# Eight starting places modulo 256 bytes for the streamed and weight tiles of an MLP

## The chip, the cores and the metric

The kernel runs on one core of a Trainium2 chip. The metric is device time in microseconds (us) for one execution. The time before is the median of three runs, 1006.82 us (1005.56 to 1008.35).

## What is computed

The reference is a linear attention with exponential features (8 batches, 8 heads, 576 tokens, head size 64, 128 features), followed by an MLP on 4608 tokens of width 512:

```python
proj = einsum('bhsd,md->bhsm', x * scale, omega)
phi  = exp(h - max(h)) / sqrt(m)         # h = proj - |x|^2 / 2, for q and for k
kv   = einsum('bhsm,bhsd->bhmd', phi(k), v)
attn = einsum('bhsm,bhmd->bhsd', phi(q), kv) / (phi(q) . sum(phi(k)) + 1e-06)
h    = x @ w_in                          # 4608 x 512 by 512 x 2048
g    = where(h > 0, h, exp(min(h, 0)) - 1)
out  = g @ w_out                         # 4608 x 2048 by 2048 x 512
```

The MLP is the larger part. To keep precision its operands are split into a high and a low part of type fp32r, and each product is computed as three: high by high, high by low, low by high.

## The kernel before, in words

Tokens are cut into 9 blocks of 512 (`TB`). The hidden width 2048 is cut into 16 slices of 128 (`NF`). A *step* is one block with one slice: `layer1` makes the slice of the hidden layer and `layer2` adds its product to the block's output. Both layers are written as products of three matmuls.

In `layer1` (from line 1000) the stationary operand, the weights that are loaded into the array, is a 128x128 piece of w1 in the buffer `w1c`; the operand that streams is 512 tokens of `xh` or `xl`, the attention's output, held in a ring of 1536 tokens. There are 4 products of three (lines 1012 to 1014), over the width 512, into one PSUM bank. ScalarE and VectorE then make `e` from it (lines 1021 to 1025), and the high and low parts of `g` are cut from `e` (helpers at lines 403 and 406). In `layer2` the stationary operand is a 128x128 piece of `g`, and what streams is a row of 512 of `w2l` or `w2h`; 4 products of three (lines 1050 to 1052) go to four banks. So each step is 24 matmuls of 512 columns, and there are 9 x 16 = 144 steps.

Where the tiles lie: `const` holds tiles of the whole run (identity, `ones`, `of`, `om`, `kvs`, then `w2h`, `w2l`, `xh`, `xl`), all of a size that is a multiple of 256 bytes in each partition. Then comes a pad of 48 floats (`GAP`), then the pool `mv` with two buffers of `w1c` and two of `g`, each 4096 bytes, then a pad of 16 floats, then the pool `sb` with all the rest, among it the tiles `tk` and `tq` (line 568 loads them as weights while `om` streams, 256 columns). A tile's start is rounded up to 32 bytes.

`weights` (line 976) fills `w1c`. In the first block's steps the weights come as 64-bit numbers and are converted by ScalarE and VectorE (`from_f64`), then stored to the scratch `w1s` in the chip's main memory (line 990); in all later blocks they are loaded from there by one DMA of 512 KB (line 993). SP's queue issues all DMAs.

The order of all the work on every engine is set ahead of time by a planner (`Plan.order`): each operation has an engine, an assumed duration and a due time, and the planner starts the one due first among those whose inputs and buffers are ready. It knows nothing of the addresses of tiles. Attention for later blocks is interleaved with the MLP of earlier ones until about 800 us; after that the MLP is alone.

Of the kernel before, what the change touches and what calls it, by code (L numbers as in the profile page):

```python
# [9 lines left out]
F32 = mybir.dt.float32  # L10
# [9 lines left out]
P = 128  # L20
# [9 lines left out]
NTT = TB // P  # L30
NBLK = NTOK // TB
RING = 3 * TB
GAP = 48
GR = 64
NJ = 9
NV = 10 * (D + 1)
# [305 lines left out]
def performer_elu_kernel(  # L342
# [39 lines left out]
    nc.vector.memset(kvs[0], 1.0)  # L382
    nc.vector.tensor_copy(ones, kvs[0])

    w2h = const.tile([P, NF, DM], F32R, name="w2h")
    w2l = const.tile([P, NF, DM], F32R, name="w2l")
    w1s = dram.tile([NF, P, 2 * NC * P], F32, name="w1s")
    part = dram.tile([NHALF * TB, DM], F32, name="part")
    turned = [dram.tile([P, NQB * NJ * QB], F32, name=f"turned{n}") for n in range(NTURN)]
    xh = const.tile([P, NC, RING], F32R, name="xh")  # L390
    xl = const.tile([P, NC, RING], F32R, name="xl")

    const.tile([P, GAP], F32, name="gap0")
    sb.tile([P, 64 - GAP], F32, name="gap1")

    pl = Plan()
    op = pl.op
# [515 lines left out]
    def from_f64(src, hi, lo, nm, due, key):  # L913

        raw = Buf(sb, [P, 2 * 512], I32, "raw", f"raw_{nm}", 3)
        u = Buf(sb, [P, 512], F32, "u", f"u_{nm}", 3)

        def words():
            return raw().rearrange("p (n w) -> p n w", w=2)

        def low():
            return words()[:, :, 0]

        def up():  # L930
            return words()[:, :, 1]

        def ui():
            return u().bitcast(I32)

        def tail():
            return u().bitcast(U16).rearrange("p (n w) -> p n w", w=2)[:, :, 0]


        op(  # L940
            "SP", 500, due - 10, lambda: nc.sync.dma_start(raw(), src), (), ((raw, 0), (raw, 1)), P * 4096,
            after=due - EARLY,
        )
        op(
            "ACT", 571, due - 7,
            lambda: nc.scalar.activation(u(), up().bitcast(F32), AF.Copy, scale=2.0 ** -112), ((raw, 1),), (u,),
        )
        op(
            "DVE", dve(512, True), due - 6,
            lambda: nc.vector.tensor_scalar(u(), u(), -F64_MAX, F64_MAX, ALU.max, ALU.min), (u,), (u,), port=True,  # L950
        )
        op(
            "DVE", dve(512, True), due - 6,
            lambda: nc.vector.tensor_scalar(ui(), ui(), 3, 0x7FFFFFFF, ALU.logical_shift_left, ALU.bitwise_and),
            (u,), (u,), port=True,
        )
        op(
            "DVE", dve(512), due - 6,
            lambda: nc.vector.scalar_tensor_tensor(ui(), up(), -(2 ** 31), ui(), ALU.bitwise_and, ALU.bitwise_or),
            (u, (raw, 1)), (u,), port=True,  # L960
        )
        op(
            "DVE", dve(512), due - 5,
            lambda: nc.vector.scalar_tensor_tensor(tail(), low().bitcast(U32), 2.0 ** -29, tail(), ALU.mult, ALU.add),  # L964
            (u, (raw, 0)), (u,),
        )
        op(
            "ACT", act(512), due - 4, lambda e: copy(e, hi(), u()), (u,), (key + ("h",),),
            alt=other("conv_hi", "DVE", dve(512, True)), port=True,
        )  # L970
        op(
            "DVE", dve(512), due - 3,
            lambda e: tt(e, lo(), u(), hi().bitcast(F32), ALU.subtract), (u, key + ("h",)), (key + ("l",),),
            alt=other("conv_sub", "POOL", pool(512)), port=True,
        )

    w1c, gt, acc = {}, {}, {}

    def weights(F, due):

        blk, f = STEPS[F][:2]
        t = w1c[F] = Buf(mv, [P, 2, NC * P], F32R, "w1c", f"w1c_{F}", 2)

        def flat():
            return t().rearrange("p a c -> p (a c)").bitcast(F32)

        both = ((t, "h"), (t, "l"))
        if blk == 0:
            from_f64(w1[f], lambda: t()[:, 0], lambda: t()[:, 1], f"w1_{f}", due, (t,))
            op("SP", 500, due, lambda: nc.sync.dma_start(w1s[f], flat()), both, (("w1s", f),), P * 4096)  # L990
            from_f64(w2[f], lambda: w2h[:, f], lambda: w2l[:, f], f"w2_{f}", due + CONV1 - (CONV2 if f < SPLIT[1] else CONV3), ("w2", f))
        else:
            op("SP", 500, due - 8, lambda: nc.sync.dma_start(flat(), w1s[f]), (("w1s", f),), both, P * 4096)

    def ring(blk):

# [2 lines left out]
    def layer1(F, due):  # L999
        blk, f = STEPS[F][:2]  # L1000
        o = (blk * TB) % RING
        w = w1c.pop(F)
        p = Buf(ps, [P, 512], F32, "pa", f"ph_{F}", 4)
        e = Buf(sb, [P, TB], F32, "e", f"e_{F}", 2)
        g = gt[F] = Buf(mv, [P, 2, TB], F32R, "g", f"g_{F}", 2)

        def ph():
            return p()[:, 0:TB]

        def mms(c):  # L1010
            wh, wl = w()[:, 0, c * P:(c + 1) * P], w()[:, 1, c * P:(c + 1) * P]
            nc.tensor.matmul(ph(), wh, xh[:, c, o:o + TB], start=(c == 0), stop=False)  # L1012
            nc.tensor.matmul(ph(), wh, xl[:, c, o:o + TB], start=False, stop=False)  # L1013
            nc.tensor.matmul(ph(), wl, xh[:, c, o:o + TB], start=False, stop=(c == NC - 1))  # L1014

        for c in range(NC):
            reads = [(z, k) for k in ring(blk) if k[1] == c for z in ("xh", "xl")]
            op("PE", mm(TB, 3), due + 0.5 * c, lambda c=c: mms(c), [*reads, (w, "h"), (w, "l")], (p,))
        due += 2

        op("ACT", act(TB, True), due, lambda: nc.scalar.activation(e(), ph(), AF.Relu, scale=-1.0), (p,), (e,))  # L1021
        op("ACT", act(TB), due + 0.2, lambda: nc.scalar.activation(e(), e(), AF.Exp, scale=-1.0), (e,), (e,))  # L1022
        op(
            "DVE", dve(TB), due + 0.8,
            lambda: nc.vector.scalar_tensor_tensor(e(), e(), -1.0, ph(), ALU.add, ALU.max), (p, e), (e,),  # L1025
        )
        first, second = ("ACT", act(TB)), ("DVE", dve(TB, True))
        if blk:
            first, second = second, first
        op(*first, due + 1.2, lambda x: copy(x, g()[:, 0], e()), (e,), ((g, 0),), alt=other("g_hi", *second), port=True)  # L1030

        first, second = ("POOL", pool(TB)), ("DVE", dve(TB))
        if not blk:
            first, second = second, first
        op(
            *first, due + 1.5,
            lambda x: tt(x, g()[:, 1], e(), g()[:, 0].bitcast(F32), ALU.subtract), (e, (g, 0)), ((g, 1),),
            alt=other("g_lo" if blk else "g_lo0", *second), port=True,
        )

    def layer2(F, due):
        blk, f, f0, f1 = STEPS[F]
        g = gt.pop(F)
        for tt in range(NTT):
            if f == f0:
                acc[tt] = Buf(ps, [P, DM], F32, f"acc{tt}", f"acc_{blk}_{f0}_{tt}", 1)

            def mms(tt=tt, a=acc[tt]):
                ts = slice(tt * P, (tt + 1) * P)
                nc.tensor.matmul(a(), g()[:, 0, ts], w2l[:, f], start=(f == f0), stop=False)  # L1050
                nc.tensor.matmul(a(), g()[:, 0, ts], w2h[:, f], start=False, stop=False)  # L1051
                nc.tensor.matmul(a(), g()[:, 1, ts], w2h[:, f], start=False, stop=(f == f1 - 1))  # L1052

            d = due + 0.65 * tt
            op("PE", 3 * 229, d, mms, ((g, 0), (g, 1), ("w2", f, "h"), ("w2", f, "l")), (acc[tt],))
            if f < f1 - 1:
                continue
            o = Buf(sb, [P, DM], F32, "u", f"o_{blk}_{f0}_{tt}", 3)
            r = blk * TB + tt * P
            if f0:  # L1060
                op("SP", 500, d - 10, lambda o=o, r=r: nc.sync.dma_start(o(), part[r:r + P]), (("part", r),), (o,), P * DM * 4)
                op(
                    "DVE", dve(DM), d,
                    lambda o=o, a=acc[tt]: nc.vector.tensor_tensor(o(), a(), o(), ALU.add), (acc[tt], o), (o,),
                )
            else:
                op(
                    "ACT", act(DM, True), d, lambda e, o=o, a=acc[tt]: copy(e, o(), a()), (acc[tt],), (o,),
                    alt=other("out", "DVE", dve(DM)),
                )  # L1070
            dst, keys = (out, ()) if f1 == NF else (part, (("part", r),))
            op("SP", 500, d + 1, lambda o=o, r=r, dst=dst: nc.sync.dma_start(dst[r:r + P], o()), (o,), keys, P * DM * 4)
# [129 lines left out]
```

## Time and profile before

| | |
|---|---|
| median of three runs | 1006.82 us (1005.56 to 1008.35) |
| the profiled execution | 1004.03 us, its span 1002.3 us |
| busy PE, VectorE (DVE), ScalarE (ACT), GpSimd (POOL) | 987.3, 708.5, 667.4, 189.6 us |
| chain that ended last | PE 86%, DVE 6%, DMA 4%, ACT 3% |
| bytes moved | 179.12 MB, 179 GB/s on the mean |

Busy time of an engine is the time with at least one of its instructions open. Matmuls overlap in the profile, since each is open from its start until its result is through, and the ends are modelled; so the sum of PE's durations is larger than its busy time, and the distance between starts says more than the duration. PEld is the loading of weights, which overlaps the matmuls. A line of a group gives the line of the code, the engine, the operation, out<-in, shapes, the count, then busy time in us and the mean duration of one in ns, then the idle time of the engine just before them and what ended it.

### The profile page before, as it was taken

The page shows a single profiled execution, that of the slowest core. Times are in us where ns is not written, and L with a number is a line of the kernel's source. Part 1 is how long each engine was busy: PE and PEld are TensorE (multiplying, and loading weights), DVE is VectorE, ACT ScalarE, POOL GpSimd, SP SyncE. Part 2 cuts the span into 40 slices and gives each one's busy share as a digit, 9 for nine tenths or more (in the row PEclk, how much of TensorE's full clock was granted, in tenths as well). Part 3 has the DMA queues.
Part 4 walks back from the last instruction along what each step waited for, and adds up shares of the span by engine and source line. Part 5 has one row for each costly group of instructions (what it writes and reads, how often), then busy time and mean ns, then how long its engine had stood idle before and what let it go on. Part 6 is the DMA issues. An engine that isn't in the chain of part 4 may idle for free.

```text
span 1002.3 us, 17185 instructions
## 1 busy us (share of the span) xinstructions
PE 987.3 (99%) x5230; PEld 805.7 (80%) x5230; DVE 708.5 (71%) x2511; ACT 667.4 (67%) x1716; POOL 189.6 (19%) x223
## 2 busy tenths in 40 slices
PE   9899999999999999999999999999999999999998
PEld 8688788787878887887788788888788778888886
DVE  6999999988887777786777776777776532333332
ACT  8988768997777777886787687777776422122222
POOL 3323201332222221222122122222122100000000
PEclk9999999999999999999999999999999999999999
DMA  8576775777666645754575556664574243324321
GB/s 202 162 228 209 240 261 195 249 249 246 221 204 197 206 146 160 250 180 144 180 242 187 175 179 208 197 206 148 165 224 153 94 125 131 100 98 134 105 85 63
DMA packets 66572, 179.12 MB, mean 179 GB/s; under 512 B 9456, under 2 KB 21936, under 8 KB 66480
## 3 DMA queue, kind: packets, MB, share of 16 engines
q1 hardware_dynamic: 66480, 178.03, 56.5%
q8 instruction: 42, 0.69, 0.3%
q14 instruction: 50, 0.41, 0.1%
HBM read 143.92 MB, written 34.08 MB: 178 GB/s over the span
## 4 chain that ended last, share of the span: by engine, by line
PE 86%; DVE 6%; DMA 4%; ACT 3%; issue 1%; POOL 0%; SPq 0%; DVEq 0%; ACTq 0%; POOLq 0%
PE ph L1012 12%; PE acc L1050 12%; PE acc L1051 12%; PE ph L1013 12%; PE acc L1052 12%; PE ph L1014 12%; PE ppq L568 2%; PE ppk L568 2%; PE pn L704 2%; PE ppq L518 1%; DMA part<-o 1%; PE ppk L518 1%; DVE u_w L964 1%; PE pkv L623 1%; ACT hk L490 1%
## 5 line engine op out<-in xcount | busy, mean ns | idle before, releaser
L1012 PE MATMUL ph<-xh,w1c 128*128 128x512 f32 x576 | 228.7, 397 | 1.2 <-DVE e L1025 1.1
L1050 PE MATMUL acc<-w2l,g 128*128 128x512 f32 x576 | 228.1, 396 | 0.0
L1013 PE MATMUL ph<-xl,w1c 128*128 128x512 f32 x576 | 226.2, 393 | 0.0
L1051 PE MATMUL acc<-w2h,g 128*128 128x512 f32 x576 | 226.0, 392 | 0.0
L1052 PE MATMUL acc<-w2h,g 128*128 128x512 f32 x576 | 225.4, 391 | 0.0
L1014 PE MATMUL ph<-xh,w1c 128*128 128x512 f32 x576 | 225.3, 391 | 0.0
L1021 ACT ACTIVATE e<-ph 128x512 f32<-128x512 f32 x144 | 85.9, 596 | 198.1 <-PE ph L1014 197.4
L1025 DVE SCALAR_TENSOR_TENSOR e<-e,ph 128x512 f32<-128x512 f32 x144 | 98.3, 683 | 110.6 <-ACT e L1022 109.6
L406 POOL TENSOR_TENSOR hq<-hq,den 128x512 f32<-128x512 f32 (+1 forms) x96 | 81.5, 860 | 288.0 <-DVE den L788 75.0
L1012 PEld LDWEIGHTS ph<-xh,w1c 128*128 128x128 f32 x576 | 108.3, 188 | 26.3 <-issue 2.7
L1014 PEld LDWEIGHTS ph<-xh,w1c 128*128 128x128 f32 x576 | 108.2, 188 | 24.5
L1052 PEld LDWEIGHTS acc<-w2h,g 128*128 128x128 f32 x576 | 108.2, 188 | 24.4
L1050 PEld LDWEIGHTS acc<-w2l,g 128*128 128x128 f32 x576 | 108.3, 188 | 21.2 <-issue 0.9
L1013 PEld LDWEIGHTS ph<-xl,w1c 128*128 128x128 f32 x576 | 108.3, 188 | 18.0
L1051 PEld LDWEIGHTS acc<-w2h,g 128*128 128x128 f32 x576 | 108.3, 188 | 18.0
L403 DVE CAST g<-e 128x512 fp32r<-128x512 f32 x128 | 55.4, 433 | 72.8 <-PE acc L1052 69.9
L406 DVE TENSOR_TENSOR g<-e,g 128x512 fp32r<-128x512 f32 x144 | 100.2, 696 | 2.0
L1022 ACT ACTIVATE e<-e 128x512 f32<-128x512 f32 x144 | 91.2, 633 | 2.8
L577 ACT ACTIVATE p2q<-ppq,sqq 128x128 f32<-128x128 f32 x216 | 66.5, 366 | 27.6 <-PE ppq L568 24.0
L788 DVE CUSTOM_DVE_ANT_0 junk<-hq,pz 128x128 f32<-128x128 f32 (+1 forms) x320 | 74.5, 280 | 6.0 <-PE pz L767 4.8
L586 DVE CUSTOM_DVE_ANT_0 hq<-ppq,p2q 128x128 f32<-128x128 f32 x216 | 54.4, 285 | 32.1 <-ACT p2q L577 31.5
L577 ACT ACTIVATE p2k<-ppk,sqk 128x128 f32<-128x128 f32 x216 | 66.6, 365 | 13.4 <-DVE mnk L586 7.6
(175 smaller groups left out, 1407.7 us busy)
## 6 DMA issues: line engine op xcount, KB each, us to landing
w1c<-w1s SPq DMA_DIRECT2D x128, 512.0 KB, 3.8
raw_w<-in_w_dram SPq DMA_DIRECT2D x32, 512.0 KB, 4.4
xk<-in_kx_dram SPq DMA_DIRECT2D x24, 576.0 KB, 5.0
xq<-in_qx_dram SPq DMA_DIRECT2D x24, 576.0 KB, 3.8
turned<-tb SPq DMA_DIRECT2D x24, 576.0 KB, 4.4
qh<-turned SPq DMA_DIRECT2D x96, 144.0 KB, 4.8
v<-in_v_dram SPq DMA_DIRECT2D x32, 325.0 KB, 5.2
out_dram<-o SPq DMA_DIRECT2D x36, 256.0 KB, 2.4
```

The costliest lines, as they stand in the source:

```text
L406: (nc.vector if e == "DVE" else nc.gpsimd).tensor_tensor(*args)
L577: nc.scalar.activation(p2()[:, a], view()[:, a, M:], AF.Identity, bias=sq()[:, j:j + 1], scale=1.0)
L788: nc.vector.tensor_tensor_reduce(out=junk()[r], in0=h()[r, j, :], in1=pz()[r, a * P:(a + 1) * P], scale=1.0, scalar=EPS, op0=ALU.mult, op1 ...
L1012: nc.tensor.matmul(ph(), wh, xh[:, c, o:o + TB], start=(c == 0), stop=False)
L1013: nc.tensor.matmul(ph(), wh, xl[:, c, o:o + TB], start=False, stop=False)
L1014: nc.tensor.matmul(ph(), wl, xh[:, c, o:o + TB], start=False, stop=(c == NC - 1))
L1021: op("ACT", act(TB, True), due, lambda: nc.scalar.activation(e(), ph(), AF.Relu, scale=-1.0), (p,), (e,))
L1022: op("ACT", act(TB), due + 0.2, lambda: nc.scalar.activation(e(), e(), AF.Exp, scale=-1.0), (e,), (e,))
L1025: lambda: nc.vector.scalar_tensor_tensor(e(), e(), -1.0, ph(), ALU.add, ALU.max), (p, e), (e,),
L1050: nc.tensor.matmul(a(), g()[:, 0, ts], w2l[:, f], start=(f == f0), stop=False)
L1051: nc.tensor.matmul(a(), g()[:, 0, ts], w2h[:, f], start=False, stop=False)
L1052: nc.tensor.matmul(a(), g()[:, 1, ts], w2h[:, f], start=False, stop=(f == f1 - 1))
```

## The change

Five pads in `const` take the place of the two pads. They stand ahead of `w2h`, between `w2h` and `w2l`, ahead of `xh`, between `xh` and `xl`, and behind `xl`. The buffers of `w1c` and `g` become flat tiles of 1048 floats (`SPAN`), 4192 bytes: the high half has the first 512, then 8 floats (`SHIFT`) are left free, then come the low half's 512, and 16 more are left free. So the low half begins 32 bytes further modulo 256 than the high one, and the second buffer 96 bytes further than the first. The DMAs of `w1c` have two pieces of 2048 bytes in each partition, where they had one of 4096. All else stays.

```diff
-GAP = 48
+SHIFT = 8
+SPAN = 2 * (512 + SHIFT) + SHIFT
...
+    def pad(n, name):
+        const.tile([P, n], F32, name=name)
+
+    pad(32, "gap0")
     w2h = const.tile([P, NF, DM], F32R, name="w2h")
+    pad(20, "gap1")
     w2l = const.tile([P, NF, DM], F32R, name="w2l")
...
+    pad(44, "gap2")
     xh = const.tile([P, NC, RING], F32R, name="xh")
+    pad(56, "gap3")
     xl = const.tile([P, NC, RING], F32R, name="xl")
-
-    const.tile([P, GAP], F32, name="gap0")
-    sb.tile([P, 64 - GAP], F32, name="gap1")
+    pad(24, "gap4")
...
+    def halves(t):
+        return t()[:, 0:2 * (512 + SHIFT)].rearrange("p (a c) -> p a c", a=2)[:, :, 0:512]
...
-        t = w1c[F] = Buf(mv, [P, 2, NC * P], F32R, "w1c", f"w1c_{F}", 2)
+        t = w1c[F] = Buf(mv, [P, SPAN], F32R, "w1c", f"w1c_{F}", 2)
...
-            op("SP", 500, due - 8, lambda: nc.sync.dma_start(flat(), w1s[f]), (("w1s", f),), both, P * 4096)
+            op("SP", 500, due - 8, lambda: nc.sync.dma_start(both_parts(), w1s[f].rearrange("p (a c) -> p a c", a=2)), (("w1s", f),), both, P * 4096)
...
-        g = gt[F] = Buf(mv, [P, 2, TB], F32R, "g", f"g_{F}", 2)
+        g = gt[F] = Buf(mv, [P, SPAN], F32R, "g", f"g_{F}", 2)
...
-            wh, wl = w()[:, 0, c * P:(c + 1) * P], w()[:, 1, c * P:(c + 1) * P]
+            wh, wl = halves(w)[:, 0, c * P:(c + 1) * P], halves(w)[:, 1, c * P:(c + 1) * P]
...
-                nc.tensor.matmul(a(), g()[:, 0, ts], w2l[:, f], start=(f == f0), stop=False)
-                nc.tensor.matmul(a(), g()[:, 0, ts], w2h[:, f], start=False, stop=False)
-                nc.tensor.matmul(a(), g()[:, 1, ts], w2h[:, f], start=False, stop=(f == f1 - 1))
+                nc.tensor.matmul(a(), halves(g)[:, 0, ts], w2l[:, f], start=(f == f0), stop=False)
+                nc.tensor.matmul(a(), halves(g)[:, 0, ts], w2h[:, f], start=False, stop=False)
+                nc.tensor.matmul(a(), halves(g)[:, 1, ts], w2h[:, f], start=False, stop=(f == f1 - 1))
```

## Rows read from the trace of the kernel before

**Rows 1.** The page: busy time of PE, and the granted clock in 40 slices.

```profile
PE 987.3 (99%) x5230; PEld 805.7 (80%) x5230; DVE 708.5 (71%) x2511; ACT 667.4 (67%) x1716; POOL 189.6 (19%) x223
...
PEclk9999999999999999999999999999999999999999
```

**Rows 2.** The page: the chain that ended last, by engine.

```profile
PE 86%; DVE 6%; DMA 4%; ACT 3%; issue 1%; POOL 0%; SPq 0%; DVEq 0%; ACTq 0%; POOLq 0%
```

**Rows 3.** Groups of PE over the whole span, by line.

```profile
L1012 PE MATMUL ph<-xh,w1c 128*128 128x512 f32 x576 | 228.7, 397 | 1.2 <-DVE e L1025 1.1
L1050 PE MATMUL acc<-w2l,g 128*128 128x512 f32 x576 | 228.1, 396 | 0.0
L1013 PE MATMUL ph<-xl,w1c 128*128 128x512 f32 x576 | 226.2, 393 | 0.0
L1051 PE MATMUL acc<-w2h,g 128*128 128x512 f32 x576 | 226.0, 392 | 0.0
L1052 PE MATMUL acc<-w2h,g 128*128 128x512 f32 x576 | 225.4, 391 | 0.0
L1014 PE MATMUL ph<-xh,w1c 128*128 128x512 f32 x576 | 225.3, 391 | 0.0
```

**Rows 4.** Timeline of PE in the tail (start, duration in us): first and last of 105.

```profile
899.62 0.39 PE L1050 MATMUL acc<-w2l,g 128*128 128x512 f32 x1
...
923.43 0.39 PE L1052 MATMUL acc<-w2h,g 128*128 128x512 f32 x1
```

**Rows 5.** Groups of PE from 820 to 980 us, the MLP alone.

```profile
L1012 PE MATMUL ph<-xh,w1c 128*128 128x512 f32 x119 | 46.6, 392 | 0.0
L1013 PE MATMUL ph<-xl,w1c 128*128 128x512 f32 x118 | 46.5, 394 | 0.0
L1014 PE MATMUL ph<-xh,w1c 128*128 128x512 f32 x119 | 46.2, 388 | 0.0
L1051 PE MATMUL acc<-w2h,g 128*128 128x512 f32 x115 | 45.3, 394 | 0.0
L1050 PE MATMUL acc<-w2l,g 128*128 128x512 f32 x115 | 45.1, 392 | 0.0
L1052 PE MATMUL acc<-w2h,g 128*128 128x512 f32 x115 | 44.6, 388 | 0.0
```

**Rows 6.** The tile w1c: durations min/median/max in ns, first and last start.

```profile
L1013 PE MATMUL ph<-xl,w1c x576: 387/394/398, 51.9 to 987.1; 128*128 128x512 f32 x192
```

**Rows 7.** Timeline of PE around a pair of L568 with attention interleaved.

```profile
702.93 0.40 PE L1052 MATMUL acc<-w2h,g 128*128 128x512 f32 x1
703.17 0.39 PE L568 MATMUL ppq<-om,tq 128*128 128x256 f32 x2
703.40 0.40 PE L1012 MATMUL ph<-xh,w1c 128*128 128x512 f32 x1
...
704.10 0.39 PE L1050 MATMUL acc<-w2l,g 128*128 128x512 f32 x1
```

**Rows 8.** Stretches: PE, PEld, DVE, ACT, POOL busy us (count), clock, DMA, GB/s.

```profile
50.00:100.00 50.00, 48.28 (x317) 41.66 (x316) 49.00 (x150) 43.21 (x111) 15.06 (x14) 1.00 0.71 218
100.00:150.00 50.00, 49.51 (x237) 39.20 (x237) 47.89 (x117) 36.27 (x75) 5.26 (x4) 1.00 0.78 250
150.00:200.00 50.00, 47.34 (x250) 38.12 (x249) 48.31 (x157) 43.30 (x108) 14.20 (x15) 1.00 0.63 221
```

**Rows 9.** Groups of PE from 50 to 250 us: one line of each layer.

```profile
L1012 PE MATMUL ph<-xh,w1c 128*128 128x512 f32 x113 | 45.8, 405 | 1.1 <-DVE e L1025 1.1
...
L1050 PE MATMUL acc<-w2l,g 128*128 128x512 f32 x101 | 40.6, 402 | 0.0
```

**Rows 10.** Line 993, the loads of w1c: SP's issue (ns), and landing.

```profile
L993 SPq DMA_DIRECT2D w1c<-w1s x128: 319/320/1404, 112.1 to 976.7; - x128
...
DMA to landing us min/median/max: 3.1/3.8/7.4
```

**Rows 11.** The page: a DMA in rows of 2048 bytes, median us to landing.

```profile
out_dram<-o SPq DMA_DIRECT2D x36, 256.0 KB, 2.4
```

More of the change, by code (lines that the diff above doesn't have):

```diff
@@ L977, in performer_elu_kernel, with both_parts @@
     w1c, gt, acc = {}, {}, {}
+    def halves(t):
+        return t()[:, 0:2 * (512 + SHIFT)].rearrange("p (a c) -> p a c", a=2)[:, :, 0:512]
     def weights(F, due):
         blk, f = STEPS[F][:2]
-        t = w1c[F] = Buf(mv, [P, 2, NC * P], F32R, "w1c", f"w1c_{F}", 2)
-        def flat():
-            return t().rearrange("p a c -> p (a c)").bitcast(F32)
+        t = w1c[F] = Buf(mv, [P, SPAN], F32R, "w1c", f"w1c_{F}", 2)
+        def both_parts():
+            return halves(t).bitcast(F32)
         both = ((t, "h"), (t, "l"))
         if blk == 0:
-            from_f64(w1[f], lambda: t()[:, 0], lambda: t()[:, 1], f"w1_{f}", due, (t,))
-            op("SP", 500, due, lambda: nc.sync.dma_start(w1s[f], flat()), both, (("w1s", f),), P * 4096)
+            from_f64(w1[f], lambda: halves(t)[:, 0], lambda: halves(t)[:, 1], f"w1_{f}", due, (t,))
+            op("SP", 500, due, lambda: nc.sync.dma_start(w1s[f].rearrange("p (a c) -> p a c", a=2), both_parts()), both, (("w1s", f),), P * 4096)
             from_f64(w2[f], lambda: w2h[:, f], lambda: w2l[:, f], f"w2_{f}", due + CONV1 - (CONV2 if f < SPLIT[1] else CONV3), ("w2", f))
         else:
-            op("SP", 500, due - 8, lambda: nc.sync.dma_start(flat(), w1s[f]), (("w1s", f),), both, P * 4096)
+            op("SP", 500, due - 8, lambda: nc.sync.dma_start(both_parts(), w1s[f].rearrange("p (a c) -> p a c", a=2)), (("w1s", f),), both, P * 4096)
     def ring(blk):
@@ L1029, in layer1 @@
             first, second = second, first
-        op(*first, due + 1.2, lambda x: copy(x, g()[:, 0], e()), (e,), ((g, 0),), alt=other("g_hi", *second), port=True)
+        op(*first, due + 1.2, lambda x: copy(x, halves(g)[:, 0], e()), (e,), ((g, 0),), alt=other("g_hi", *second), port=True)
         first, second = ("POOL", pool(TB)), ("DVE", dve(TB))
@@ L1036, in layer1 @@
             *first, due + 1.5,
-            lambda x: tt(x, g()[:, 1], e(), g()[:, 0].bitcast(F32), ALU.subtract), (e, (g, 0)), ((g, 1),),
+            lambda x: tt(x, halves(g)[:, 1], e(), halves(g)[:, 0].bitcast(F32), ALU.subtract), (e, (g, 0)), ((g, 1),),
             alt=other("g_lo" if blk else "g_lo0", *second), port=True,
```

## The prediction

> **What bounds the kernel now.** I began with the busy shares. TensorE is busy 987.3 of 1002.3 us and its granted clock is 9 tenths or more in every slice (1.00 in each stage of [rows 8]), which is the level of 2.4 GHz [rows 1]; the other engines have room. The chain that ended last lies on PE for 86% [rows 2]. So the time is the sum of what PE issues, and only what one matmul costs, or how many there are, can move it.
>
> Next I read PE's groups [rows 3]. The six lines of the MLP (three products in each layer) have 576 matmuls of 512 columns each, 3456 in all, and their busy time is over 1350 us, more than the span: matmuls overlap in this profile, so a mean duration is not what one costs. The cost is the distance from start to start. In the undisturbed tail two starts lie 899.62 and 923.43 us, with 104 matmuls from the one to the other [rows 4]: 23.81/104 = 228.9 ns each. The mean duration in the tail is (392 + 394 + 388 + 392 + 394 + 388)/6 = 391.3 ns [rows 5]. So the cost is the duration less about 162.4 ns, and durations may stand for costs: 388 is a matmul of 225.6 ns, 394 one of 231.6 ns. The reader is to see here that matmuls of one shape, at one clock, with nothing to wait for, are *not* alike: they come in three steps, and the same line always gets the same step within this stage. Over the whole run one line's matmuls lie between 387 and 398 ns with a median of 394 [rows 6]. Something in how the operands are read makes up to 11 ns of difference.
>
> That place in memory may be that something is seen at L568. All first-generation buffers of the constants, om and the tiles tk and tq among them, begin at one place modulo 256 bytes; w1c and g begin 192 bytes further (the pad of 48 floats), and a second pad of 16 brings the other tiles back. So every MLP matmul streams from one place while the weights of the next are loaded from a place 192 bytes on, but when an L568 follows, its weights lie at the very place of the stream. At 702.93 such a pair shows: 0.24 us from the matmul's start to the start of L568, and the matmul itself reads 0.40 where the steady ones read 0.39; the three matmuls after the pair of L568 take 704.10 - 703.40 = 0.70 us, or 233 ns each, against 228.9 [rows 7]. By the code there are 24 pairs x 2 x 9 = 432 matmuls of L568.
>
> **The change, part by part.**
>
> *Places.* The allocator rounds a tile up to 32 bytes, so the pads of 32, 20, 44, 56 and 24 floats are 128, 96, 192, 224 and 96 bytes. Counted from w2h: w2h 0, w2l 96, xh 32, xl 0; the two buffers of w1c 96 and 192, their low halves 32 further; those of g 32 and 128, low halves 32 further; om 128, and tk and tq 224. What counts, if place counts, is the distance from the stream to the weights that come next. Before it is 192 for all. After, inside a product of three, it is 192 and 64 (then 32 to the next) with g's first buffer, 32 and 160 (then 128) with its second; 64 and 128 with w1c's first, 160 and 224 with its second. None is 0. From L1014 to a layer-2 product it is 0 with g's first buffer, and for L568 it becomes 96. The trace shows the distances 192 and 0 for streams of 512 and nothing of 32, 64, 96, 128, 160 or 224, so the price of the new ones is bounded from both sides. Cheap end: every matmul at the cheapest step, 388 against the run's mean of (397 + 396 + 393 + 392 + 391 + 391)/6 = 393.3 ns [rows 3, 5], -5.3 ns. Dear end: every one at 397.5, the step beside L568 and close to the longest one seen, 398 [rows 6, 7], +4.2 ns. I take the middle between today's mean and the cheap end, -2.65 ns. Reason: what distance 0 does beside L568 is the dear step, distances of 0 all but vanish, and mixed distances break the pattern in which two of three steps are above the cheapest. This is the weakest step of the sum; no row prices the new distances.
>
> *How much of it reaches the end.* From 50 to 200 us DVE is busy 49.0, 47.9 and 48.3 of 50 us, and PE has gaps already [rows 8]. There DVE hides any gain of PE, though not a loss. The MLP has about 3 x 113 + 3 x 101 = 642 matmuls from 50 to 250 us [rows 9]; I drop them all. That leaves 2814 x 2.65 = 7.5 us.
>
> *Copies of w1c.* Each row of 4096 contiguous bytes becomes two of 2048 on the side of the chip's memory, in 16 stores and 128 loads; bytes and number of DMAs stay. SP's issue is 320 ns (median) and a load lands in 3.8 us, 7.4 at worst [rows 10]. SP can issue the load only when the buffer comes free, as one step's layer 1 ends and it is wanted when the next but one begins. A step is 24 matmuls, 24 x 228.9 = 5.5 us, so cover is about 5.5 us against 3.8. PE's wait ahead of L1012 is 1.2 us in the whole run and none of it is a DMA's [rows 3]. I cost it at nothing; if a load took twice as long, 7.6 us, about 2 us would be lost in each of the 128 steps, 256 us. From the rows, 256 KB in rows of 2048 bytes land in 2.4 us [rows 11], so a doubling is far off. SP stores 16 more chunks likewise; who stands behind them on SP is the next load, with the same cover.
>
> *Vector and scalar engines.* The same instructions write g and read e at other places; nothing is added. In the stage where DVE binds, a change of 1% in its time would be 0.01 x 145 = 1.5 us either way. I take 0. The order of the work is fixed by a planner that knows nothing of places, so no queue is reordered.
>
> *Sum.* The profiled execution took 1004.03 us, 2.79 below the median of 1006.82. 1004.0 - 7.5 = 996.5 against that execution, and 999.3 us against the median.
>
> **The rivals.**
>
> *No difference.* The three steps might come from PE's own issue and have nothing to do with places; then all places are alike. For it: the steps follow one another in a fixed order whatever the line, in both layers alike [rows 5], though these read different tiles. Against it: L568, above. It also comes out so if gains and losses over eight distances cancel, or if the builder drops pads that nobody uses (before has two such pads). Time: 1006.8. The Trainium skill, in "SBUF — State Buffer", section "Who interferes with whom", speaks for this case: it gives PE two independent read ports, one for the moving operand and one for weight loads, and says that PE never waits on anyone. By that rule the change would be worth 0 us; the 11 ns between the shortest and the longest matmul of one line [rows 6] are not explained by it.
>
> *Slower: the new distances are worse than 192.* Place: every MLP matmul, all stages. If 192 is already a good distance, most of seven others are worse. Price: halfway to the dear step, 2.1 ns x 3456 = 7.3 us, 1014.1; all the way, 4.2 x 3456 = 14.5 us, 1021.3. It decides from the point where the mean duration of the six lines is above 393.3 ns. For it: 192 stays for few kinds of pairs, and with 192 one step in three is already the cheapest. Against: of the two distances that can be seen, the other one is dear. A late w1c load (above) is a second way to this side, with little chance.
>
> *A larger gain.* If the overhead over the bare stream went altogether, the gain would pass the cheap end. Against it: no matmul of 576 on a line is under 387 ns [rows 6], and two streams of 256 columns with two weight loads (703.17 to 703.40, 0.23 us) cost as much as one of 512 [rows 7], so the overhead goes with the columns rather than with the loads. From 393.3 down to 387 on all 3456 would be 21.8 us, 985. The Trainium skill, "TensorE: Matmul & The Clock Gate", section "Back-to-back issue gap", gives N/2.4 + 2.5 ns for a warm matmul, 215.8 ns at 512 columns; the trace does not agree, at 228.9 ns. By the page's figure, as an estimate, 3456 x (230.9 - 215.8) = 52 us would be there to win, 955 us.
>
> **How the numbers follow.** A measurement of this kernel can tell about 0.3%, 3 us, from no change (three runs here lie within 2.8 us). Forecast of a gain by better distances: 0.42, own range 988.5 (5.3 ns on all 3456, 18.3 us) to 1003.8. Larger gain: 0.04. No difference: 0.24. Worse distances: 0.27, and late loads 0.03. So faster 0.46, same 0.24, slower 0.30. The range goes from 987, just past the cheap end, to 1015, just past half of the dear end; it leaves out the larger gain, the upper half of the slower case and late loads.
>
> **What would show it.** In the changed kernel's tail, the mean durations of the six lines should no longer be 388, 392 and 394 but mostly 386 to 390, unequal between the two buffers, and the start-to-start mean near 226 to 227 ns; the matmul ahead of an L568 should no longer read 0.40. PE's wait ahead of L1012 should stay near 1 us and w1c's landing near 3.8 us. Tail means above 392 would make the forecast wrong and the slower rival right; the same 388, 392 and 394 would show that place does not matter.

## The result and the profile after

The changed kernel takes 1015.25 us (median of five runs, 1013.27 to 1017.03) where the kernel before takes 1006.82; the ratio is 1.0085 with a 95% interval of 1.0057 to 1.0112. It is slower by 8.4 us, clear of the measurement.

The page of the changed kernel: busy PE, then the six lines of the MLP (L1021 to L1023 were L1012 to L1014, L1059 to L1061 were L1050 to L1052).

```profile
PE 998.1 (99%) x5230; PEld 809.1 (80%) x5230; DVE 709.3 (70%) x2511; ACT 667.7 (66%) x1716; POOL 189.2 (19%) x223
...
L1021 PE MATMUL ph<-xh,w1c 128*128 128x512 f32 x576 | 229.8, 399 | 2.1 <-DVE e L1034 1.0
L1059 PE MATMUL acc<-w2l,g 128*128 128x512 f32 x576 | 229.4, 398 | 0.0
L1023 PE MATMUL ph<-xh,w1c 128*128 128x512 f32 x576 | 227.6, 395 | 0.0
L1061 PE MATMUL acc<-w2h,g 128*128 128x512 f32 x576 | 227.1, 394 | 0.0
L1022 PE MATMUL ph<-xl,w1c 128*128 128x512 f32 x576 | 227.0, 394 | 0.0
L1060 PE MATMUL acc<-w2h,g 128*128 128x512 f32 x576 | 226.7, 394 | 0.0
```

PE's busy time rose by 10.8 us and that of VectorE, ScalarE and GpSimd by less than 1 us [rows 1]. The mean duration of the six lines is now (399 + 398 + 395 + 394 + 394 + 394)/6 = 395.7 ns, against 393.3 [rows 3]: 2.4 ns on each of 3456 matmuls, 8.3 us. PE's wait ahead of layer 1 rose by 0.9 us only, 0.8 us of it for one load of `w1c`.

The tail shows it with nothing else around. Groups of PE of the changed kernel from 820 to 980 us, then two rows of its timeline (start, duration in us) with 105 matmuls from the one to the other:

```profile
L1023 PE MATMUL ph<-xh,w1c 128*128 128x512 f32 x115 | 45.3, 394 | 0.0
L1022 PE MATMUL ph<-xl,w1c 128*128 128x512 f32 x115 | 45.2, 393 | 0.0
L1021 PE MATMUL ph<-xh,w1c 128*128 128x512 f32 x115 | 45.1, 392 | 0.0
L1059 PE MATMUL acc<-w2l,g 128*128 128x512 f32 x113 | 44.7, 395 | 0.0
L1061 PE MATMUL acc<-w2h,g 128*128 128x512 f32 x113 | 44.5, 393 | 0.0
L1060 PE MATMUL acc<-w2h,g 128*128 128x512 f32 x113 | 44.4, 393 | 0.0
```

```profile
879.68 0.39 PE L1021 MATMUL ph<-xh,w1c 128*128 128x512 f32 x1
...
903.94 0.39 PE L1059 MATMUL acc<-w2l,g 128*128 128x512 f32 x1
```

(903.94 - 879.68)/105 = 231.0 ns, where it was 228.9 [rows 4], and the ordered steps of 388, 392 and 394 [rows 5] have become means of 392 to 395 on all lines. So the time went into the matmuls themselves: the same number, of the same shape, at 2.1 to 2.4 ns more each.

The two profiled executions differ by a little more, 1013.0 against 1002.3 us of span. One other thing can be seen: in the stretches (columns as in [rows 8]) the changed kernel's granted clock is 0.66 on the mean from 60 to 65 us, so for most of this stretch it was at the lower level of 1.2 GHz. Ahead of it PE had stood idle for 2.39 us, up to 59.83.

```profile
60.00:65.00 5.00, 5.00 (x21) 4.30 (x22) 4.84 (x25) 4.26 (x10) 2.38 (x2) 0.66 0.40 84
```

That is 5 x 0.34 = 1.7 us of work lost in this execution. It is no part of the change. Most later profiles have such a dip (a mean clock of 0.998), the kernel that only splits copies among them, and that one is as fast as before. Executions of the kernel before have it too (a mean of 0.997 in two of the seven beside the run `gap_24` below).

### The profile page after: what moved, and what is told of

It reads as the page before. It is cut to its first block, busy times and chain, and to the rows that moved or that the text cites. A ratio compares the mean times of both kernels' runs of the same rounds, so it can differ in the third digit from the quotient of the medians.

```text
span 1013.0 us, 17185 instructions
## 1 busy us (share of the span) xinstructions
PE 998.1 (99%) x5230; PEld 809.1 (80%) x5230; DVE 709.3 (70%) x2511; ACT 667.7 (66%) x1716; POOL 189.2 (19%) x223
## 2 busy tenths in 40 slices
DMA packets 85004, 179.12 MB, mean 177 GB/s; under 512 B 9456, under 2 KB 21936, under 8 KB 84912
## 4 chain that ended last, share of the span: by engine, by line
PE 90%; DVE 5%; DMA 3%; ACT 2%; issue 1%; POOL 0%; DVEq 0%; ACTq 0%; POOLq 0%
PE ph L1021 13%; PE acc L1059 12%; PE ph L1023 12%; PE ph L1022 12%; PE acc L1061 12%; PE acc L1060 12%; PE ppk L574 2%; PE ppq L574 2%; PE pn L710 2%; PE ppq L524 2%; PE ppk L524 2%; PE pkv L629 1%; DVE junk L794 1%; DMA w1c<-w1s 1%; DMA raw_w<-in_w_dram 1%; DMA xk<-in_kx_dram 1%
## 5 line engine op out<-in xcount | busy, mean ns | idle before, releaser
L1021 PE MATMUL ph<-xh,w1c 128*128 128x512 f32 x576 | 229.8, 399 | 2.1 <-DVE e L1034 1.0
L1059 PE MATMUL acc<-w2l,g 128*128 128x512 f32 x576 | 229.4, 398 | 0.0
L1023 PE MATMUL ph<-xh,w1c 128*128 128x512 f32 x576 | 227.6, 395 | 0.0
L1061 PE MATMUL acc<-w2h,g 128*128 128x512 f32 x576 | 227.1, 394 | 0.0
L1060 PE MATMUL acc<-w2h,g 128*128 128x512 f32 x576 | 226.7, 394 | 0.0
L1021 PEld LDWEIGHTS ph<-xh,w1c 128*128 128x128 f32 x576 | 108.6, 189 | 28.4 <-issue 3.0
L1023 PEld LDWEIGHTS ph<-xh,w1c 128*128 128x128 f32 x576 | 108.5, 188 | 25.5
L1061 PEld LDWEIGHTS acc<-w2h,g 128*128 128x128 f32 x576 | 108.3, 188 | 25.5
L1059 PEld LDWEIGHTS acc<-w2l,g 128*128 128x128 f32 x576 | 108.2, 188 | 21.3 <-issue 0.9
```

What stands on the lines that cost most here:

```text
L1059: nc.tensor.matmul(a(), halves(g)[:, 0, ts], w2l[:, f], start=(f == f0), stop=False)
L1060: nc.tensor.matmul(a(), halves(g)[:, 0, ts], w2h[:, f], start=False, stop=False)
L1061: nc.tensor.matmul(a(), halves(g)[:, 1, ts], w2h[:, f], start=False, stop=(f == f1 - 1))
```

## The experiments

Four theories at first. *Theory 1*: each distance from the stream to the weights that come next has its price. *Theory 2*: a mixture of distances costs by itself. *Theory 3*: starts that are no multiple of 64 bytes cost. *Theory 4*: the copies in two pieces cost. The *distance* of a pair of matmuls is the place of the second one's weights less the place of the first one's stream, modulo 256 bytes.

### Copies alone (split_copies)

```diff
-        t = w1c[F] = Buf(mv, [P, 2, NC * P], F32R, "w1c", f"w1c_{F}", 2)
+        t = w1c[F] = Buf(mv, [P, 2 * 576], F32R, "w1c", f"w1c_{F}", 2)
...
+        return t().rearrange("p (a c) -> p a c", a=2)[:, :, 0:512]
```

> The kernel before, with the two halves of w1c 256 bytes further apart: all places modulo 256 bytes stay, and each w1c copy has rows of 2048 bytes as after the change. Theory 4 (the copies cost): 1013 to 1015 us, with more waits ahead of the first matmul of layer 1. Theories 1 to 3 (places cost): 1006.8 within 3 us, the tail's mean duration stays at 391.3 ns, 18432 more packets.

Measured: 1007.04 us, ratio 1.0005 (0.9991 to 1.0018), 85004 packets like the changed kernel. The tail's steps are untouched; the loads' landing is 3.9 us.

```profile
L1016 PE MATMUL ph<-xl,w1c 128*128 128x512 f32 x118 | 46.5, 394 | 0.0
L1015 PE MATMUL ph<-xh,w1c 128*128 128x512 f32 x118 | 46.3, 392 | 0.0
L1017 PE MATMUL ph<-xh,w1c 128*128 128x512 f32 x117 | 45.4, 388 | 0.0
```

Theory 4 falls. What remains lies in the places.

### Half of the change each (pads_only, buffers_only)

```diff
-SHIFT = 8
+SHIFT = 0
```

> The changed kernel with its five pads, but w1c and g as before (halves and buffers at one place): distances 64 and 96 in layer 1, 0 and 96 in layer 2, the same in every step. Theory 1: set by the prices of 0, 64 and 96; by the changed kernel's own pairs (230.9, 231.0, 233.5 ns) about 232 ns, 1014 to 1016 us. Theory 2: few distances in a fixed order, so between 229 and 231.9 ns, 1007 to 1012 us. Theory 3: streams at 32 and 96 and all weights at 96 are odd multiples of 32, so the full loss, 1014 us or more.

```diff
-    pad(32, "gap0")
-    pad(20, "gap1")
-    pad(44, "gap2")
-    pad(56, "gap3")
-    pad(24, "gap4")
+    pad(48, "gap0")
```

> The changed kernel without its pads ahead of and between the four streamed tiles (one pad of 48 floats behind them, as before): all streams at one place, halves and buffers of w1c and g at places 32 and 96 bytes apart, so distances 192, 224, 32, 64 in layer 1 and 128, 160, 224, 0 in layer 2. Theory 1: the mean of these prices, which the scan gives. Theory 2: as mixed as the changed kernel, 231.5 to 232 ns per matmul, 1013 to 1016 us. Theory 3: half of the weights are odd and no stream is, so about half the loss, 1010 to 1012 us.

Measured: the pads alone 1012.38 us, 1.0053 (1.0034 to 1.0072); the halves and buffers alone 1013.57 us, 1.0072 (1.0057 to 1.0087). From start to start the tail has 231.6 ns with the pads and 232.3 with the buffers. Each half of the change brings most of the loss, and they don't add up. Theory 3 wanted about half the loss from the second; it had nearly all. Between theories 1 and 2 these runs do not decide: theory 1's time for the pads (1014 to 1016 us) was missed by 1.6 us, theory 2's (1007 to 1012 us) by 0.4, and theory 2's for the buffers held.

### Eight distances in one tail (scan_tail)

```diff
+    def place(F):
+        return 8 * ((F - 112) // 4) if F >= 112 else 0
+
+    def halves(t, F):
+        return t()[:, place(F):place(F) + 1024].rearrange("p (a c) -> p a c", a=2)
```

> The kernel before, with room in the buffers of w1c and g so that, in the last 32 steps alone (from about 820 us, the MLP alone), both begin 32 bytes further every 4 steps: the distance from the stream to the weights is 192, 224, 0, 32, 64, 96, 128, 160 in turn, the same for all matmuls of a step. Theory 1 (each distance has its price): the eight stretches differ, 192 near 229 ns per matmul, others up to 233 to 236, mean of all about 231. Theory 2 (it is the mixture of distances that costs, not any one of them): all eight stretches stay at 229 within 0.5 ns, with dearer matmuls only where two distances meet. Theory 3 (starts that are no multiple of 64 bytes cost): 192, 0, 64 and 128 at 229, the other four at 231 or more. The time is that of before within 3 us in all three.

Measured, from start to start within the part of each stretch where all matmuls have one distance (18 matmuls or more):

| distance modulo 256 | 192 | 224 | 0 | 32 | 64 | 96 | 128 | 160 |
|---|---|---|---|---|---|---|---|---|
| ns per matmul | 228.9 | 233.2 | **226.7** | 233.3 | 233.3 | 234.1 | 232.8 | 233.3 |

Three of these from the timeline of PE: distance 0 (22 matmuls from the first row to the last), 96 (21) and 160 (42).

```profile
876.01 0.40 PE L1058 MATMUL acc<-w2h,g 128*128 128x512 f32 x1
...
881.01 0.39 PE L1059 MATMUL acc<-w2h,g 128*128 128x512 f32 x1
...
943.34 0.39 PE L1019 MATMUL ph<-xh,w1c 128*128 128x512 f32 x1
...
948.25 0.40 PE L1057 MATMUL acc<-w2l,g 128*128 128x512 f32 x1
...
988.08 0.39 PE L1019 MATMUL ph<-xh,w1c 128*128 128x512 f32 x1
...
997.88 0.39 PE L1057 MATMUL acc<-w2l,g 128*128 128x512 f32 x1
```

4.91/21 = 233.8 and 9.80/42 = 233.3 ns; the first stretch, with its entry, 5.00/22 = 227.3. Theory 2 in its pure form falls, since a single distance of 96 or 160 is dear all by itself, and theory 3 falls with 64 and 128. The distance that the prediction held to be dear, 0, is the cheapest of all, and 192 is the only other cheap one among the eight.

### A bad distance throughout (gap_24)

```diff
-GAP = 48
+GAP = 24
```

> The kernel before with the pads 24 and 40 floats instead of 48 and 16: every MLP stream at distance 96 from the next weights, the same throughout, all other tiles where they are. If the distance is what costs (the scan of the tail had 234 ns at 96): tail at 234 ns, 5 more than before; with about half of that where attention is interleaved, 850 x 5 + 2600 x 2.5 = 10.8 us, so 1014 to 1019 us, as slow as the changed kernel or slower without any mixture of places. If the mixture is needed for the loss: 1006 to 1008 us, tail at 229.

Measured: 1018.31 us, ratio 1.0128 (1.0106 to 1.015). Timeline of PE, 103 matmuls: 24.13/103 = 234.3 ns, as in the scan.

```profile
879.80 0.40 PE L1052 MATMUL acc<-w2h,g 128*128 128x512 f32 x1
...
903.93 0.39 PE L1012 MATMUL ph<-xh,w1c 128*128 128x512 f32 x1
```

One number in the kernel before, and no mixture at all, gives a loss larger than that of the whole change. The 2.5 ns that were expected where attention is interleaved were too few: from 300 to 800 us a matmul (waits left out) took 233.6 ns, against 229.9 before.

### Distance 0 throughout (gap_0, gap_64)

```diff
-    const.tile([P, GAP], F32, name="gap0")
     sb.tile([P, 64 - GAP], F32, name="gap1")
```

(with `GAP = 0`; the other keeps the first line, with `GAP = 64`, and drops the second)

> The kernel before with the pad of 48 floats made 64 (256 bytes) and the second pad dropped: the distance from every MLP stream to the next weights is 0 modulo 256 (256 bytes modulo 512), all other tiles stay where they are. Theory 1 as the scan refined it (each distance has a steady price: 0 is 226.7 ns, 192 is 228.9, the other six 232.8 to 234.1): 2.2 ns less on each of 3456 matmuls, 7.6 us, so about 999 us, tail at 226.7 ns. Theory 2b (the 226.7 holds only where nothing else comes between; pairs of L568 and the other products of attention throw the matmuls out of it): gain only in the tail, 850 x 2.2 = 1.9 us, about 1005 us.

> The same with no pad ahead of the buffers (the second pad 64 floats): distance 0 modulo 512 too. Theory 1 with a period of 256 bytes: as the pad of 64, 999 us, tail at 226.7 ns. Theory 5 (the period is longer than 256 bytes): another tail mean, 229 to 234 ns, and 1007 to 1020 us.

Measured: 1001.94 us for the pad of 0, ratio 0.9961 (0.9947 to 0.9975); 1002.78 us for the pad of 64, 0.9969 (0.9958 to 0.9981). Both beat both kernels. Groups of PE with the pad of 0, three lines from 820 to 980 us, then two from 300 to 800 us:

```profile
L1051 PE MATMUL acc<-w2h,g 128*128 128x512 f32 x118 | 45.9, 389 | 0.0
L1011 PE MATMUL ph<-xh,w1c 128*128 128x512 f32 x118 | 45.9, 389 | 0.0
L1012 PE MATMUL ph<-xl,w1c 128*128 128x512 f32 x118 | 45.9, 389 | 0.0
```

```profile
L1049 PE MATMUL acc<-w2l,g 128*128 128x512 f32 x296 | 117.1, 396 | 0.0
...
L1051 PE MATMUL acc<-w2h,g 128*128 128x512 f32 x296 | 115.4, 390 | 0.0
```

In the tail all six lines have the same 389 ns: the three steps are gone, and the start-to-start mean is 226.7 ns with either pad, so nothing here needs a period longer than 256 bytes. Half of the expected gain is missing, because it comes in full only in the tail. From 300 to 800 us a matmul (waits left out) costs 229.2 ns against 229.9 before: 850 x 2.2 + 1740 x 0.7 = 3.1 us, and the first 300 us bring about 0.9 ns on 770 matmuls, 0.7 us more. That is 3.8 us, and 0.39% of 1005 is 3.9. The sum is one of matmul costs, not of spans: the profiled execution with the pad of 0 was the slowest of its ten (1005.39 us), its MLP began 2.6 us later than in the profile before (54.1 against 51.5 us), and its span is the longer one of the two, 1003.6 against 1002.3 us.

The timeline shows where the gain goes. With the pad of 0, behind and ahead of L567 (L568 of the kernel before):

```profile
641.66 0.28 PE L567 MATMUL ppk<-om,tk 128*128 128x256 f32 x1
641.78 0.40 PE L1049 MATMUL acc<-w2l,g 128*128 128x512 f32 x1
...
642.94 0.39 PE L1013 MATMUL ph<-xh,w1c 128*128 128x512 f32 x1
...
647.70 0.39 PE L1051 MATMUL acc<-w2h,g 128*128 128x512 f32 x1
647.92 0.64 PE L567 MATMUL ppq<-om,tq 128*128 128x256 f32 x4
```

The first five matmuls behind L567 take 1.16/5 = 232 ns, the next 21 take 4.76/21 = 226.7. Over all of 300 to 800 us (starts of the timeline, waits left out) the first ten matmuls of the MLP behind one of attention cost 230.3 ns on the mean, in this kernel as in the one before; those further on cost 226.7 here and 229.1 there. So the gain is made by the matmuls further on alone, 499 of 1731.

### Is it the distance of L568? (tk_192)

```diff
-    const.tile([P, GAP], F32, name="gap0")
-    sb.tile([P, 64 - GAP], F32, name="gap1")
+    sb.tile([P, GAP], F32, name="gap1")
```

> The kernel with the pad of 0, and the pad ahead of the other tiles 48 floats instead of 64: w1c and g at distance 0, but tk and tq (the weights of the 432 matmuls of 256 columns, L568 of the kernel before) at 192 from the streams. In the run with the pad of 0 the matmuls between 300 and 800 us cost 229.2 ns against 226.7 in the tail. If the pairs of L568 at distance 0 throw the next product out of its cycle and 192 does not: half of it comes back, about 230 ns to 228, 999 us. If any stream of 256 columns does it, whatever the distance: as with the pad of 0, 1001 to 1002 us, or 1 to 3 us more.

Measured: 1003.65 us, ratio 0.997 (0.9952 to 0.9988), no better than the pad of 0 alone. From 300 to 800 us:

```profile
L1049 PE MATMUL acc<-w2l,g 128*128 128x512 f32 x297 | 117.5, 396 | 0.0
...
L1051 PE MATMUL acc<-w2h,g 128*128 128x512 f32 x297 | 116.2, 391 | 0.0
```

The same 396 for the first matmul of a product, 391 instead of 390 for the last. So a change of distance there brings nothing. The first ten matmuls behind an interruption cost 230.7 ns here and those further on 226.7: it is the interruption by attention's streams, at either distance, that throws the matmuls out of their cheap cycle. What in it does so was not tried apart.

### Mixtures (scan_fine, scan_halves, layers_apart)

```diff
+        if F < 120:
+            return 16 * (F % 2)
+        return (16, 17, 18, 20, 12, 4)[(F - 120) // 4]
```

> The tail scan again, with other stretches: in its first 8 steps the two buffers differ (distance 192 in even steps, 0 in odd ones), then 4 steps each at distances 0, 4, 8, 16, 240 and 208. Theory 1 (steady prices): the first stretch lies between 226.7 and 228.9, at 227.8 ns; 0 at 226.7 again. Theory 2 (a mixture costs by itself): the first stretch is dearer than either price, 230 to 232 ns. For the fine distances the theories say nothing; if the price follows the overlap of 32-byte blocks, 4, 8 and 16 stay near 227, and 240 and 208 are near 233.

Measured: with the two buffers at 192 and 0, 80 matmuls of the timeline take 18.23 us, 227.9 ns, which is the mean of the two prices.

```profile
833.62 0.39 PE L1024 MATMUL ph<-xl,w1c 128*128 128x512 f32 x1
...
851.85 0.39 PE L1023 MATMUL ph<-xh,w1c 128*128 128x512 f32 x1
```

Two cheap distances mixed *between* products cost nothing that can be seen; the distance changes only three times in 24 matmuls there. The fine distances: 0 again 226.7 ns, 240 also 226.7, 4 gives 232.2, 8 gives 230.8, 16 and 208 give 233.3. The guess about 32-byte blocks missed; four bytes are enough to lose 5.5 ns.

```diff
+        return ((0, 8), (16, 8), (8, 8), (12, 4))[(F - 112) // 8] if F >= 112 else (0, 0)
...
+        o, d = place(F)
+        return t()[:, o:o + 2 * (512 + d)].rearrange("p (a c) -> p a c", a=2)[:, :, 0:512]
```

> The tail scan with the low halves of w1c and g apart from the high ones, as the change has it (32 bytes; 16 in the last stretch), 8 steps each: distances inside a product of three (192, 224, 192), (0, 32, 0), (224, 0, 224), (240, 0, 240). Theory 1 (each pair pays the steady price of its distance): 230.4, 228.9, 231.1 and 226.7 ns. If a mixture inside a product costs by itself (mixtures between products did not): all four above these by 1 ns or more.

Measured: about 231.1, 233.3, 233.3 and 233.3 ns. The timeline of the second stretch (0, 32, 0; 87 matmuls) and of the last (240, 0, 240; 82):

```profile
879.68 0.40 PE L1058 MATMUL acc<-w2l,g 128*128 128x512 f32 x1
...
899.98 0.40 PE L1020 MATMUL ph<-xh,w1c 128*128 128x512 f32 x1
...
975.75 0.40 PE L1060 MATMUL acc<-w2h,g 128*128 128x512 f32 x1
...
994.88 0.40 PE L1058 MATMUL acc<-w2l,g 128*128 128x512 f32 x1
```

20.30/87 and 19.13/82 are 233.3 ns both. *Inside* a product of three a mixture does cost: 240 and 0 are 226.7 each alone and 233.3 together. But there the distance changes twice in three matmuls, so the place of the change and how often it comes were not told apart. In three of four stretches the pair prices were missed by 2.2 to 6.6 ns, in the first by less than 1.

```diff
-GAP = 48
+GAP = 24
...
+    const.tile([P, GAP], F32, name="gap0")
     w2h = const.tile([P, NF, DM], F32R, name="w2h")
...
+    const.tile([P, 64 - GAP], F32, name="gap1")
     xh = const.tile([P, NC, RING], F32R, name="xh")
...
-        g = gt[F] = Buf(mv, [P, 2, TB], F32R, "g", f"g_{F}", 2)
+        g = gt[F] = Buf(mv, [P, 1024 + 64], F32R, "g", f"g_{F}", 2)
...
+        return t()[:, GAP:GAP + 1024].rearrange("p (a c) -> p a c", a=2)
```

> Layer 1's tiles (xh, xl, w1c) at one place, layer 2's (w2h, w2l, g) 96 bytes further: the distance is 0 inside all products of a layer, and 96 or 160 only where a product of one layer follows one of the other, 701 of the 3455 pairs. Theory 1 (steady prices by distance; what a tile's own place is does not matter): (2754 x 226.7 + 701 x 233.7)/3455 = 228.1 ns in the tail, some 1.4 ns more than with the pad of 0, so about 1006 us, far from the changed kernel's 1015. If the places themselves matter (tiles that begin at 224 or at 128 modulo 256), or a change of distance upsets more than its own pair: 230 ns or more in the tail, 1010 us or more.

Measured: 1010.48 us, ratio 1.0045 (1.0027 to 1.0064), and in the tail 105 matmuls take 24.27 us, 231.1 ns instead of 228.1.

```profile
879.63 0.40 PE L1055 MATMUL acc<-w2h,g 128*128 128x512 f32 x1
...
903.90 0.40 PE L1017 MATMUL ph<-xh,w1c 128*128 128x512 f32 x1
```

The pairs at distance 0 in this kernel take 230.9 ns on the mean over the whole run, not 226.7. That is no matter of the tiles' own places. At the end of this run layer 2 is alone, with streams and weights 96 bytes further than those of layer 1, and there 35 matmuls take 7.94/35 = 226.9 ns:

```profile
997.03 0.39 PE L1053 MATMUL acc<-w2l,g 128*128 128x512 f32 x1
...
1004.97 0.39 PE L1055 MATMUL acc<-w2h,g 128*128 128x512 f32 x1
```

So a dear pair upsets those behind it: from 820 us on, the first eight pairs at distance 0 behind a change of layer cost 230.7 ns on the mean, those further on 226.8 (48 of them, most at the end). The run also tells which weights count. In it every matmul's stream lies at distance 0 from that matmul's own weights; what changes with the layer is the place of the next weights and of the next stream. If the own weights alone counted, all would cost 226.7 ns.

**What follows.** Theory 1 stands as far as a kernel with one distance goes (226.7 ns at 0 and 240, 228.9 at 192, 231 to 234 at all others that were tried), and it is not additive: what a pair costs depends on the pairs ahead of it. The change put eight distances in the place of 192, of which only 0 and 192 itself are cheap (16% of its pairs), and mixed them inside products. By the steady prices alone, weighted with the changed kernel's pairs, its matmuls would cost 232.5 ns; they cost 231.0 in the tail. Why some distances are cheap is not settled: no run shows the mechanism behind them.

## Why the prediction was wrong

The forecast was a gain, and the result is a loss, 0.25 us past the upper end of the range (1015), in the rival "the new distances are worse than 192".

*What bounds the kernel.* Right. The time is PE's, the cost of a matmul is what moved, and durations less about 162 ns followed the starts: 393.3 - 231.0 = 162.3 in the changed tail.

*Places.* Here it failed: "I take the middle between today's mean and the cheap end, -2.65 ns". The measured term is +2.4 ns. The step's reason, "what distance 0 does beside L568 is the dear step", read a cause into a coincidence. L568 has distance 0, and it is also a stream of 256 columns that breaks the sequence. With the pad of 0 the distance ahead of an L568 is still 0, and the matmul there takes 227.1 ns on the mean (300 to 800 us, 133 of them; 647.92 - 647.70 = 0.22 us in the rows above), where it took 232.3 before. The run with L568 at 192 shows that the matmuls behind it are as dear at that distance, and the scan that no distance is cheaper than 0. The "dear end" of 397.5 ns was read at the same place, so it too was no price of a distance. The other reason, "mixed distances break the pattern in which two of three steps are above the cheapest", was half true: they broke it, and the steps came out dearer. One distance had been measured in the trace before, and it was a good one; seven unknown ones should have been given a price from both sides with the middle near no gain, or above.

*The slower rival.* Its place, its price and its point were right: halfway to the dear step was worked out as 2.1 ns on 3456 matmuls, 1014.1 us; measured were 2.4 ns and 1015.25 us, and the mean of the six lines is above 393.3 ns. That the size came out is in part luck: the dear step was read beside L568, and halfway to it rested on no row. "If 192 is already a good distance, most of seven others are worse" is what the scan shows.

*No difference.* Excluded: the ratio's interval lies above 1. The rule of the Trainium skill that was weighed for it ("SBUF — State Buffer", section "Who interferes with whom", by which PE's reads of stream and weights have ports of their own and PE waits for no one) does not cover what was measured: moving the weights' tiles by 96 bytes, and nothing else, takes a matmul from 226.7 to 234.3 ns.

*A larger gain.* Nothing went below 226.7 ns in a steady stretch; the cheap end of 225.6 was not reached by any layout.

*DVE hides a gain from 50 to 200 us.* Not tested apart. The prediction counted on it for a gain alone, so it has no part in the loss.

*Copies of w1c.* Costed at nothing, and split_copies shows that (1.0005). In the changed kernel's profile one load came 0.8 us late, and with the pad of 0, where copies are whole, one came 0.7 us late. But SP's issue did not stay at 320 ns, as the last section tells.

*What would show it.* The signs named for the slower rival came: the tail's mean is 393.3 ns, above 392, and the steps 388, 392 and 394 are gone. The landing of w1c stayed at 3.9 us.

## What to carry to other kernels

Where PE is busy all the time, compare matmuls of one shape: if they come in steps with nothing to wait for, the place of the weights relative to the stream is worth a scan, and one run can try many distances if only the last steps of the kernel move their buffers. Keep one good distance for all matmuls, rather than many: here one at 0 gained 0.4%, one at 96 lost 1.3%, and eight places lost 0.8%. A price read beside another kind of matmul is not that of the distance until the two are taken apart.

## What had not been expected

A DMA whose rows are in two pieces takes SP longer to issue: 524 ns against 320 [rows 10]. From the kernel that only splits copies, line 996:

```profile
L996 SPq DMA_DIRECT2D w1c<-w1s x128: 517/524/1481, 115.6 to 980.6; - x128
```

Over 128 loads that is 26 us more of SP's time, all hidden.

Four bytes of distance were worth 5.5 ns on a matmul of 227 (0 against 4), and 240 is as good as 0 while 224 and 208 are within 1 ns of the worst, 96. At one distance the costs also come in a fixed, repeating order: at 160, the steps from start to start were 231, 232 and 237 ns over and over. Three of them take 700 ns, as on the mean at 16, 32, 64 and 208; at 0 and 240 three take 680.
